# Loading one piece of a weight matrix as 120 and 8 rows, and another in one transfer, in a DMA-bound decode kernel

## The chip, the cores and the metric

The kernel runs on one core of a Trainium2 chip. The metric is the device time of one execution in microseconds (us). A profiled execution also has a span, from its first to its last instruction; the span is about 1.8 us shorter than the time.

## The reference, cut to what matters

One decode step of a gated mix: attention over a window of the cached keys and values, a small MLP, and a gate between them.

```python
# x (8, 1, 448); k_cache, v_cache (8, 8, 4096, 256); wq (448, 4096); wo (4096, 448)
q = (x @ wq)                              # 16 heads of 256
scores = q k^T / 16 over the last 1024 keys, softmax, o = p v
a = o.reshape(8, 1, 4096) @ wo            # the output projection
b = gelu(layernorm(x) @ w1 + b1) @ w2 + b2
return g * a + (1 - g) * b                # g = sigmoid(sum(x * gate_w))
```

The kernel has to read 77.7 MB of keys, values and weights from HBM, the chip's main memory. The output weights `wo` (4096 x 448 bf16, 3.67 MB) are used last.

## The kernel before

All large loads go, in a fixed order, through a ring of nine slots in SBUF, the on-chip memory; a slot is a tile of 128 partitions with 16 KB in each. One queue (SyncE) issues them. `wo` comes last, in two slots of two quarters each. A quarter has 128 rows, one per partition, of 8 columns j with 448 numbers each: 7168 B per row. `WO_PARTS` says in which pieces of j a quarter is loaded; later quarters are cut finer, so that the last matmuls wait for less.

```python
WO_PARTS = [[(0, 4), (4, 8)]] * 2 + [[(0, 4), (4, 6), (6, 8)]] * 2
...
def pump():                       # fills the ring as slots come free
    while len(slots) < min(len(plan), consumed[0] + RING):
        t = ring.tile([P, SLOT], BF16, tag="slot", name="slot")
        plan[len(slots)](t)
        slots.append(t)
...
def rows_loader(pieces):
    def load(t):
        o = 0
        for ap in pieces:
            ...                   # n = numbers per row of this piece
            dst = t[:, o : o + n]
            ...
            nc.sync.dma_start(dst, ap)
            o += n
    return load
...
wo_v = A_wo.rearrange("(q p j) n -> p q (j n)", p=P, j=NJ8)
for q in range(0, NHQ, 2):
    add(("wo", q), rows_loader(
        [wo_v[:, q + i, j0 * D : j1 * D] for i in range(2) for j0, j1 in WO_PARTS[q + i]]))
...
def project(q):                   # 24 matmuls per quarter, 3 per column j
    w = slot("wo", q - q % 2)
    for j in range(NJ8):
        o = ((q % 2) * NJ8 + j) * D
        for dst, cols in tiles(A_ps):
            nc.tensor.matmul(dst, lhsT=oP[:, j, q, :],
                             rhs=w[:, o + cols.start : o + cols.stop], ...)
```

## Time and profile before

| | before |
|---|---|
| median time, the 3 runs known at first | 190.32 us (190.27 to 190.78) |
| span of the profiled execution | 188.7 us |
| HBM read | 77.68 MB, 412 GB/s over the span |
| last landing of the output weights | 185.47 us |

The next lines are from the page of the kernel before: the span, the busy time of the compute engines (PE is TensorE's matmuls, PEld its weight loads, DVE VectorE, ACT ScalarE, POOL GpSimd), the DMA engines' busy tenths and the rate they moved in 40 equal slices, and the summary of the chain that ended last.

```profile
span 188.7 us, 2420 instructions
...
PE 134.0 (71%) x975; PEld 69.5 (37%) x975; DVE 128.0 (68%) x186; ACT 43.3 (23%) x91; POOL 5.0 (3%) x7
...
DMA  6999999999999999999999999999999999999990
GB/s 217 412 427 430 433 427 431 438 427 427 431 431 434 431 431 427 431 431 431 431 431 432 427 431 424 434 434 434 420 431 441 431 424 427 438 434 418 406 377 29
...
DMA 89%; DVE 5%; PE 4%; issue 0%; ACT 0%; SPq 0%
DMA slot<-in_A_k_cache_dram 39%; DMA slot<-in_A_wo_dram 20%; DMA slot<-in_A_v_cache_dram 20%; DMA slot<-in_B_w_dram 6%; DMA slot<-in_A_wq_dram 4%; DVE kt L358 4%; PE S L430 2%; DVE mx L442 1%; PE PO L502 1%; PE fin L532 0%; DVE ET L472 0%; DVE res L691 0%; PE mz L450 0%; DVE os__969 L517 0%; PE A_ps L673 0%
...
```

The DMA engines are busy from the second slice to the second last, at some 430 GB/s. The compute engines are not near their limit. The chain is 89% DMA.

The end of the chain in order of time (start, length, what):

```profile
...
147.47 31.34 DMA slot<-in_A_wo_dram
178.81 0.02 issue
178.83 6.65 DMA slot<-in_A_wo_dram
185.47 0.04 issue
185.52 0.33 PE A_ps L673 x5
185.84 0.03 issue
185.87 0.38 DVE res L691
```

The last landing (185.47 us) releases the last matmuls, then one VectorE instruction, then the stores. So the time is set by the slowest of the DMA engines in the last transfers. TensorE's timeline shows the same (start, length, line, shape, count, and in brackets its idle time and what ended it):

```profile
...
181.68 2.27 PE L673 MATMUL A_ps<-slot,oP 128*8 128x144 bf16 x48
184.43 0.83 PE L673 MATMUL A_ps<-slot,oP 128*8 128x160 bf16 x18 [0.48 <-DMA slot<-in_A_wo_dram]
185.52 0.30 PE L673 MATMUL A_ps<-slot,oP 128*8 128x160 bf16 x6 [0.26 <-DMA slot<-in_A_wo_dram]
```

The page gives a mean over 16 DMA engines. In the trace a transfer of 128 rows has 16 landings on its semaphore, which I take as one per engine. For the last piece of `wo` the trace has them at these times in us:

```
183.39 183.62 183.63 183.77 183.87 183.97 184.00 184.33 184.59 184.80 184.97 185.00 185.01 185.03 185.09 185.47
```

The engines finish over 2.1 us, and the last is 0.38 us behind the next. The trace's DMA packet records carry no engine number. But nearly every packet starts 3 to 4 ns before another one ends (4912 of the 4935 that start between 30 and 180 us), so they can be chained into 16 lanes, which I take for the 16 engines. Seven lanes are late (they end their data at 184.51 to 185.19 us, the others at 183.07 to 184.02 us), and they are the seven that carried one 16 KB instruction fetch each (0.88 to 0.97 us).

### The profile page before, as it was taken

What the parts mean: (1) busy time and instruction counts of PE and PEld (TensorE: products, weight loads), DVE (VectorE), ACT (ScalarE), POOL (GpSimd) and SP (SyncE); (2) the same over time, 40 slices, a digit from 0 to 9 for tenths busy, and PEclk for the clock granted to TensorE, in tenths of its full rate; (3) what the DMA queues carried; (4) which work ended last, traced back from release to release, by engine and by line L of the source; (5) the groups of instructions that cost most, each with busy time, mean ns of one, the idle gap of its engine ahead of it and who ended that gap; (6) DMA issues with size and microseconds to landing.
All of it is one profiled execution on the core that took longest, in us unless ns stands there. A gap on an engine that the chain in (4) does not pass through costs nothing.

```text
span 188.7 us, 2420 instructions
## 1 busy us (share of the span) xinstructions
PE 134.0 (71%) x975; PEld 69.5 (37%) x975; DVE 128.0 (68%) x186; ACT 43.3 (23%) x91; POOL 5.0 (3%) x7
## 2 busy tenths in 40 slices
PE   0056789795848875699758599959693999397592
PEld 0022754342414342344333153515241534144281
DVE  7841498997949492949494949585867777695210
ACT  2032400214130404022404004401240043135200
POOL 8100000000000000000000000000000000000000
PEclk9999658999996999759999657988999579999758
DMA  6999999999999999999999999999999999999990
GB/s 217 412 427 430 433 427 431 438 427 427 431 431 434 431 431 427 431 431 431 431 431 432 427 431 424 434 434 434 420 431 441 431 424 427 438 434 418 406 377 29
DMA packets 7293, 77.84 MB, mean 412 GB/s; under 512 B 993, under 2 KB 1650, under 8 KB 2546
## 3 DMA queue, kind: packets, MB, share of 16 engines
q1 hardware_dynamic: 7088, 77.67, 97.0%
q8 instruction: 7, 0.11, 0.2%
q10 hardware_dynamic: 194, 0.02, 0.1%
q14 instruction: 4, 0.03, 0.0%
HBM read 77.68 MB, written 0.01 MB: 412 GB/s over the span
## 4 chain that ended last, share of the span: by engine, by line
DMA 89%; DVE 5%; PE 4%; issue 0%; ACT 0%; SPq 0%
DMA slot<-in_A_k_cache_dram 39%; DMA slot<-in_A_wo_dram 20%; DMA slot<-in_A_v_cache_dram 20%; DMA slot<-in_B_w_dram 6%; DMA slot<-in_A_wq_dram 4%; DVE kt L358 4%; PE S L430 2%; DVE mx L442 1%; PE PO L502 1%; PE fin L532 0%; DVE ET L472 0%; DVE res L691 0%; PE mz L450 0%; DVE os__969 L517 0%; PE A_ps L673 0%
## 5 line engine op out<-in xcount | busy, mean ns | idle before, releaser
L358 DVE STREAM_TRANSPOSE kt<-slot 128x2048 int32<-128x2048 int32 x32 | 73.7, 2305 | 32.1 <-DMA slot<-in_A_k_cache_dram 32.1
L430 PE MATMUL S<-kt,qw 128*128 128x512 bf16 x256 | 70.1, 420 | 29.1 <-DVE kt L358 26.4
L430 PEld LDWEIGHTS <-qw 128*128 128x128 bf16 x256 | 26.4, 103 | 68.4 <-issue 47.1
L459 ACT ACTIVATE E<-S,nmx 128x1024 bf16<-128x1024 f32 x16 | 22.2, 1390 | 3.2 <-DVE nmx L456 3.2
L535 ACT CAST oT<-fin 128x16 bf16<-128x16 f32 x16 | 3.6, 227 | 76.3 <-PE fin L532 76.3
L502 PE MATMUL PO<-slot,ET 128*16 128x512 bf16 x256 | 19.8, 437 | 1.4 <-DMA slot<-in_A_v_cache_dram 1.4
L442 DVE TENSOR_REDUCE mx<-S 128x1 f32<-128x1024 f32 x16 | 18.9, 1184 | 0.0
L511 ACT ACTIVATE first<-PO,own 128x256 f32<-128x256 f32 x16 | 7.6, 474 | 30.1 <-PE PO L502 30.1
L424 PE MATMUL S<-place,foreign 128*128 128x512 bf16 x32 | 13.1, 410 | 0.1
L472 DVE STREAM_TRANSPOSE ET<-E 128x512 int32<-128x512 int32 x16 | 11.2, 697 | 2.2 <-ACT E L459 2.2
L450 PE MATMUL mz<-m,same 128*128 128x4 f32 x32 | 6.6, 278 | 4.1 <-ACT oT L535 4.1
L483 PEld LDWEIGHTS den<-rowsum,rowden 128*128 128x128 f32 x32 | 7.3, 232 | 3.7 <-issue 1.4
L502 PEld LDWEIGHTS <-ET 128*16 128x16 bf16 x256 | 5.5, 93 | 6.5 <-issue 3.1
L450 PEld LDWEIGHTS mz<-m,same 128*128 128x128 f32 x32 | 5.5, 211 | 6.0 <-ACT oT L535 5.3
L424 PEld LDWEIGHTS <-foreign 128*128 128x128 bf16 x32 | 3.2, 101 | 9.4 <-issue 7.6
L483 PE MATMUL den<-rowsum,rowden 128*128 128x1 f32 x32 | 5.3, 235 | 0.4 <-ACT E L459 0.4
L673 PE MATMUL A_ps<-slot,oP 128*8 128x144 bf16 (+1 forms) x96 | 4.5, 301 | 0.8 <-DMA slot<-in_A_wo_dram 0.7
L494 ACT ACTIVATE rsel<-sel,rb 128x8 f32<-128x8 f32 x16 | 4.7, 296 | 1.1 <-DVE rb L493 1.1
L415 DVE CAST qw<-qp 32x512 bf16<-32x512 f32 x4 | 2.7, 687 | 3.1 <-ACT qw L413 3.1
L293 POOL MEMSET qw<- 128x5120 bf16 x1 | 4.4, 4366 | 0.0
L391 DVE COPY qd<-qt 128x64 bf16<-128x64 bf16 x4 | 0.6, 217 | 5.1 <-PE qt L387 5.1
L444 DVE TENSOR_SCALAR m<-block,mx 128x4 f32<-128x4 f32 x16 | 3.7, 229 | 0.6
(135 smaller groups left out, 86.9 us busy)
## 6 DMA issues: line engine op xcount, KB each, us to landing
slot<-in_A_v_cache_dram SPq DMA_DIRECT2D x16, 2048.0 KB, 37.0
slot<-in_A_k_cache_dram SPq DMA_DIRECT2D x15, 2048.0 KB, 36.6
slot<-in_A_wo_dram SPq DMA_DIRECT2D x6, 448.0 KB, 31.3
slot<-in_A_wq_dram SPq DMA_DIRECT2D x1, 2048.0 KB, 7.6
slot<-in_A_k_cache_dram SPq DMA_DIRECT2D x2, 1024.0 KB
slot<-in_B_w_dram SPq DMA_DIRECT2D x1, 1568.0 KB
slot<-in_B_w_dram SPq DMA_DIRECT2D x1, 1344.0 KB, 11.8
slot<-in_A_wq_dram SPq DMA_DIRECT2D x1, 1024.0 KB
```

The source lines that it names most:

```text
L358: nc.vector.transpose(kt[:].rearrange("p c k x r -> p (c k x r)").bitcast(WORD), kn[:, hf * CH * Dh : (hf + 1) * CH * Dh].bitcast(WORD),)
L424: nc.tensor.matmul(S[u][:, cols], lhsT=foreign[:], rhs=place[:], start=True, stop=False)
L430: nc.tensor.matmul(S[u][:, cols], lhsT=qw[:, j, u, m * RQ : m * RQ + P], rhs=kt[:, :, k, :, par], start=False, stop=(k == NK - 1 and par = ...
L442: nc.vector.reduce_max(mx[:], S[u][:], axis=AXIS.X)
L450: nc.tensor.matmul(mz[:], lhsT=same[:], rhs=m4[:], start=True, stop=True)
L459: nc.scalar.activation(E[:].rearrange("p c x i -> p c i x"), S.pop(u)[:].rearrange("p (c i x) -> p c i x", i=PAIR, x=BLK), ACT.Exp, bias=n ...
L472: nc.vector.transpose(ET[:].rearrange("p c r i -> p (c r i)").bitcast(WORD), E[:].rearrange("p c x i -> p (c x i)").bitcast(WORD),)
L483: nc.tensor.matmul(den[u][:], lhsT=rowden[:], rhs=rowsum[:], start=True, stop=True)
L494: nc.scalar.activation(rsel[u][:], sel2[:], ACT.Copy, scale=rb[:])
L502: nc.tensor.matmul(PO[32 * t : 32 * t + PAIR * RQ], lhsT=ET[:, c, 0:RQ, :], rhs=vn[:, PAIR * c * Dh : PAIR * (c + 1) * Dh], start=(c < QUA ...
L511: nc.scalar.activation(first[:], PO[:, 0, :], ACT.Copy, scale=own[:, 0:1])
L673: nc.tensor.matmul(dst, lhsT=oP[:, j, q, :], rhs=w[:, o + cols.start : o + cols.stop], start=(q == 0 and j == 0), stop=(q == NHQ - 1 and j ...
```

## The change

Its intent, as I read it: the DMA engines do not finish together (2.1 us apart in the trace above). The 120-row transfer and the 8-row transfer I take to use 15 engines and 8; the cut spares the sixteenth engine its share of one piece, in the hope that this one ends last. The first quarter in one transfer keeps the number of `wo` transfers at ten.

```diff
-    WO_PARTS = [[(0, 4), (4, 8)]] * 2 + [[(0, 4), (4, 6), (6, 8)]] * 2
+    WO_PARTS = [[(0, 8)], [(0, 4), (4, 8)]] + [[(0, 4), (4, 6), (6, 8)]] * 2
...
-    def rows_loader(pieces):
+    def rows_loader(pieces, cut=None):
         def load(t):
             o = 0
-            for ap in pieces:
+            for i, ap in enumerate(pieces):
...
-                nc.sync.dma_start(dst, ap)
+                for r0, r1 in ((0, P - 8), (P - 8, P)) if i == cut else ((0, P),):
+                    nc.sync.dma_start(dst[r0:r1], ap[r0:r1])
...
-                ]
+                ],
+                cut=4 if q else None,
```

The piece that is cut is columns 4 and 5 of the last quarter (224 KB). The last piece, columns 6 and 7, stays whole.

## The prediction

> **What bounds the kernel.** DMA. The page's slice view has the 16 DMA engines at 9 tenths or more in 38 of 40 slices, mostly at 405 to 440 GB/s. The chain that ended last is 89% DMA. The output weights' landings are its last stretch, until 185.5 us; then 0.33 us of matmuls (L673), 0.38 us for the result (L691) and the stores; the span is 188.7 us.
>
> **The tail, from the packet records.** A transfer of 128 rows has 16 landings, one per DMA engine. For the last weight piece they come from 183.39 us to ... 184.97, 185.00, 185.01, 185.03, 185.09 and, alone, 185.47 us. The last matmuls need all 16: one engine is 0.38 us behind the next. I chained the packet records into 16 lanes (a packet starts 3 to 4 ns before its lane's last one ends). The seven late lanes are the seven that each carried one 16 KB instruction fetch (0.88 to 0.97 us, with slower packets around it). The latest lane also had the slowest first packet (1.69 us; most 1.0 to 1.3). Lanes never even out: the queue stays full to the end. The records do not name engines. [...]
>
> **What the change does.** [...] engine 15 is spared its 8 packets of 1792 B. Here these follow each other every 70.5 ns: with a completion record near 0.57 us. [...]
>
> First quarter in one transfer: two packets of 3584 B per row (136.5 ns each) become one of 7168 B. Estimate from 159, 309 and 611 ns for 4, 8 and 16 KB: 271 ns; with the saved completion record 0.05 us less per engine. It mainly keeps the number of weight transfers at 10. The last issue waits for an earlier completion and comes about 1 us later (near 179.9 us), with 3 us or more still queued on every engine: free. The first projection starts at 180.5 us, after its weights landed anyway. No compute instruction changes.
>
> **Worth.** All on the critical path only if engine 15 is the laggard. Then the last landing falls back to the next lane: 0.38 + 0.05 = about 0.43 us less. Otherwise: 0.05 less to 0.03 more. That the cut spares exactly engine 15, by a bit more than the lag, makes me give 70% to the first. Predicted: 190.0 us (before 190.32), 0.2% less; range 189.5 to 190.5, widened for the scatter of before (190.27 to 190.78). Chances: faster by over 2% 0.01; within 2% 0.98; slower 0.01.
>
> **What the profile would show.** Right: 15 landings for the 120-row piece and 8 for the 8-row piece; the last piece's final landing near 185.05 us and no longer alone (under 0.15 us after the next); the first projection does not wait for weights; 7168 B packets take about 271 ns. Wrong: the lone last landing stays, near 185.4 us.
>
> **What would make it wrong.** The laggard changes from run to run (slow first packets, rotating instruction fetches), so sparing one engine helps less on average; 120 rows take fewer than 15 engines; the narrower transfer slows its packets.

"Engine 15" is only my name for the engine that gets no row of the cut piece; no record carries an engine number. The sum came to 0.38 + 0.05 = 0.43 us less if that engine was the last one. Of the other case, 0.05 us less to 0.03 us more, the upper end is, less the 0.05 us, one more packet for each engine that gets one of the 8 rows besides its share of the 120, 0.076 us (an estimate from 70.5 ns to the next packet and 5.5 ns for a completion record, in the trace of before). The predicted 190.0 us, 0.32 us less, lies between the two cases.

## The result

| | before | changed |
|---|---|---|
| median of 4 runs each | 190.30 us (190.24 to 190.78) | 190.97 us (190.81 to 191.24) |
| span of the profiled execution | 188.7 us | 189.0 us |
| last landing of the output weights | 185.47 us | 185.78 us |

The ratio is 1.0031, with a 95% interval of 1.0011 to 1.0052: slower by 0.3%, clear of noise, where 0.2% less was predicted. All ratios here are the mean time of one kernel's fast runs over that of the other's of the same rounds, so not quite the ratio of the medians. (The profiled execution of before, 190.53 us, was one of its slower ones, and the changed kernel's, 190.81 us, its fastest; so the two traces differ by less than the medians.)

The same lines of the changed kernel's page:

```profile
span 189.0 us, 2420 instructions
...
PE 127.9 (68%) x975; PEld 66.4 (35%) x975; DVE 127.8 (68%) x186; ACT 43.2 (23%) x91; POOL 5.0 (3%) x7
...
DMA  6999999999999999999999999999999999999990
GB/s 223 403 427 433 428 432 440 427 420 427 444 440 413 427 440 437 413 433 433 444 433 404 433 440 440 409 433 440 437 427 416 437 440 437 406 437 426 410 353 31
...
DMA 93%; PE 4%; DVE 1%; issue 0%; ACT 0%; SPq 0%
DMA slot<-in_A_k_cache_dram 60%; DMA slot<-in_A_wo_dram 23%; DMA slot<-in_B_w_dram 6%; DMA slot<-in_A_wq_dram 4%; PE S L432 3%; DVE kt L360 1%; PE PO L504 1%; PE A_ps L675 0%; PE fin L534 0%; DVE res L693 0%; PE mz L452 0%; PE S L426 0%; ACT oT L537 0%; PE den L485 0%; SPq L119 0%
...
```

Little has moved except in the 39th slice: 353 GB/s instead of 377. The chain's end:

```profile
...
142.29 36.20 DMA slot<-in_A_wo_dram
178.49 0.02 issue
178.51 7.07 DMA slot<-in_A_wo_dram
185.58 0.04 issue
185.62 0.53 PE A_ps L675 x9
186.15 0.02 issue
186.18 0.38 DVE res L693
```

And TensorE's timeline:

```profile
...
181.56 1.98 PE L675 MATMUL A_ps<-slot,oP 128*8 128x144 bf16 x48
184.65 0.44 PE L675 MATMUL A_ps<-slot,oP 128*8 128x160 bf16 x12 [1.11 <-DMA slot<-in_A_wo_dram]
185.62 0.50 PE L675 MATMUL A_ps<-slot,oP 128*8 128x160 bf16 x12 [0.53 <-DMA slot<-in_A_wo_dram]
```

The last two waits for weights are longer (1.11 and 0.53 us instead of 0.48 and 0.26). By the landings of the trace the first of them ends with the last quarter's first piece (184.61 us) and the second with the 8 rows of the cut piece (185.58 us). The VectorE instruction after them takes 0.38 us as before. The first projection, in both kernels, did not wait for weights.

The windows of the tail show the rate. The columns are the stretch, its length, the busy time of PE, PEld, DVE, ACT and POOL with instruction counts, the granted clock, the DMA engines' busy share and, last, GB/s. Before:

```profile
...
182.00:184.00 2.00, 1.95 (x45) 1.77 (x40) 0.28 (x1) 0.00 (x0) 0.00 (x0) 0.55 0.89 346
184.00:186.00 2.00, 1.03 (x24) 0.54 (x23) 0.13 (x1) 0.00 (x0) 0.00 (x0) 1.00 0.17 66
...
```

Changed:

```profile
...
182.00:184.00 2.00, 1.54 (x42) 1.40 (x37) 0.16 (x1) 0.00 (x0) 0.00 (x0) 0.73 0.94 314
184.00:186.00 2.00, 0.82 (x24) 0.48 (x23) 0.00 (x0) 0.00 (x0) 0.00 (x0) 1.00 0.28 95
...
```

From 182 to 184 us the changed kernel moves 314 GB/s instead of 346, while its DMA engines are called busier (0.94 instead of 0.89). The packets take longer. That is directly visible in the packet records: a packet of 1792 B normally takes 74 ns, one of 3584 B 140 ns. In the changed kernel 143 of the 242 data and completion packets that start between 183 and 186 us are slow: over 80 ns with 1792 B, over 150 ns with 3584 B, or over 12 ns for a completion, which normally takes 9 ns. Most of the slow data packets take 80 to 120 ns and 175 to 250 ns. In the kernel before, none is slow in that stretch. Summed over all lanes from 181 us on, the excess of the data packets over their normal times is 5.5 us, against 0.8 us before (the latter lies next to instruction fetches). The slow packets are in all lanes that still load, also in those still at an uncut piece.

The lanes of the changed kernel also tell which one is the sixteenth engine, because only that one has no packet of the cut piece. It ended its data at 182.85 us, before every other lane; the last ended at 185.27 us. With the eight packets that it was spared (0.57 us, an estimate from 70.5 ns from one to the next) it would have ended near 183.42 us, still before all others. It carried no 16 KB instruction fetch. So the engine that was spared had nothing to be relieved of.

### The profile page after: what moved, and what is told of

The parts are those of the page before. It is cut to its first block, busy times and chain, and to the rows that moved or that the text cites. A ratio compares the mean times of both kernels' runs of the same rounds, so it can differ in the third digit from the quotient of the medians.

```text
span 189.0 us, 2420 instructions
## 1 busy us (share of the span) xinstructions
PE 127.9 (68%) x975; PEld 66.4 (35%) x975; DVE 127.8 (68%) x186; ACT 43.2 (23%) x91; POOL 5.0 (3%) x7
## 4 chain that ended last, share of the span: by engine, by line
DMA 93%; PE 4%; DVE 1%; issue 0%; ACT 0%; SPq 0%
DMA slot<-in_A_k_cache_dram 60%; DMA slot<-in_A_wo_dram 23%; DMA slot<-in_B_w_dram 6%; DMA slot<-in_A_wq_dram 4%; PE S L432 3%; DVE kt L360 1%; PE PO L504 1%; PE A_ps L675 0%; PE fin L534 0%; DVE res L693 0%; PE mz L452 0%; PE S L426 0%; ACT oT L537 0%; PE den L485 0%; SPq L119 0%
## 5 line engine op out<-in xcount | busy, mean ns | idle before, releaser
L432 PE MATMUL S<-kt,qw 128*128 128x512 bf16 x256 | 67.5, 409 | 34.7 <-DVE kt L360 31.9
L504 PE MATMUL PO<-slot,ET 128*16 128x512 bf16 x256 | 18.3, 410 | 1.5 <-DMA slot<-in_A_v_cache_dram 1.5
L485 PEld LDWEIGHTS den<-rowsum,rowden 128*128 128x128 f32 x32 | 6.5, 207 | 3.2 <-issue 1.1
L452 PEld LDWEIGHTS mz<-m,same 128*128 128x128 f32 x32 | 5.0, 195 | 5.9 <-ACT oT L537 5.3
```

The costliest lines, as they stand in the source:

```text
L432: nc.tensor.matmul(S[u][:, cols], lhsT=qw[:, j, u, m * RQ : m * RQ + P], rhs=kt[:, :, k, :, par], start=False, stop=(k == NK - 1 and par = ...
L452: nc.tensor.matmul(mz[:], lhsT=same[:], rhs=m4[:], start=True, stop=True)
L485: nc.tensor.matmul(den[u][:], lhsT=rowden[:], rhs=rowsum[:], start=True, stop=True)
L504: nc.tensor.matmul(PO[32 * t : 32 * t + PAIR * RQ], lhsT=ET[:, c, 0:RQ, :], rhs=vn[:, PAIR * c * Dh : PAIR * (c + 1) * Dh], start=(c < QUA ...
```

## The experiments

Theory A: the 120-row transfer slows the packets of all engines while it is in flight, and sparing an engine that is early gains nothing. Rivals: B, the merged first quarter and the later issues; C, chance, the laggard differing by execution; D, the 8-row transfer; later E (a cost for each odd transfer, whatever its bytes), F (a cost only in the tail) and a rival that blames the reading of the source.

In e4, theory A is taken to hold for other row counts than 128 in general. "Destination theory" stands for the supposition that the cause lies where the engines write.

### The two halves of the change, and the 8 rows

e1 has only the merged quarter:

```diff
-                cut=4 if q else None,
+                cut=None,
```

> Only the first quarter in one transfer, no cut (9 weight transfers). Theory A (the 120-row transfer is the cause: it slows the packets of every DMA engine while it is in flight): 190.2 to 190.3 us, as before or 0.05 us less; no packet of 1792 or 3584 B in the last 4 us is slower than its usual 74 or 140 ns outside lanes with an instruction fetch. Rival B (the merged transfer and the later issues are the cause): 190.9 us or more. Rival C (chance: which engine lags differs from execution to execution): 190.3 us, with another spread of the last landings than before.

e2 has only the cut:

```diff
-    WO_PARTS = [[(0, 8)], [(0, 4), (4, 8)]] + [[(0, 4), (4, 6), (6, 8)]] * 2
+    WO_PARTS = [[(0, 4), (4, 8)]] * 2 + [[(0, 4), (4, 6), (6, 8)]] * 2
```

> Only the cut into 120 and 8 rows, first quarter in two transfers as before (11 weight transfers). Theory A: 190.9 to 191.1 us, with the slow packets (about 97 ns for 1792 B, 195 ns for 3584 B) from about 183 us on in all lanes still loading, and the last landing 0.4 to 0.5 us after the last data packet. Rival B: 190.3 us, no slow packets.

e3 is the changed kernel with the piece whole and the 8-row transfer beside it:

```diff
-                for r0, r1 in ((0, P - 8), (P - 8, P)) if i == cut else ((0, P),):
-                    nc.sync.dma_start(dst[r0:r1], ap[r0:r1])
+                nc.sync.dma_start(dst, ap)
+                if i == cut:
+                    nc.sync.dma_start(t[P - 8 : P, 2 * NJ8 * D : 2 * NJ8 * D + n], ap[P - 8 : P])
```

> The changed kernel with the piece uncut (128 rows), but with the 8-row transfer kept beside it: the same 8 rows are loaded a second time, into unused columns of the same slot (result unchanged). Theory A: as e1, at most 0.1 us more for 8 packets of 1792 B, 190.2 to 190.4 us, no slow packets. Rival D (the 8-row transfer, 8 engines writing 8 neighbouring partitions, is the cause): 190.8 to 191.1 us with slow packets from the moment the 8-row packets run.

e4 cuts at 112 rows:

```diff
-                for r0, r1 in ((0, P - 8), (P - 8, P)) if i == cut else ((0, P),):
+                for r0, r1 in ((0, P - 16), (P - 16, P)) if i == cut else ((0, P),):
```

> The changed kernel with the piece cut at 112 rows: 112 and 16 rows, both over 16 engines. Theory A [...]: 190.8 to 191.1 us with slow packets, although no engine is spared. Form A2 (only the 15-engine transfer does it): 190.3 us, no slow packets.

Measured, against 11 runs of before in the same rounds (median 190.49 us):

| run | median us | ratio (95% interval) | packet excess from 181 us on, all lanes | last landing |
|---|---|---|---|---|
| e1 merge only | 190.39 | 0.9995 (0.9982 to 1.0008) | 0.6 us | 185.53 |
| e2 cut only | 191.30 | 1.0055 (1.0023 to 1.0087) | 4.3 us | 186.02 |
| e3 8 rows beside | 190.55 | 1.0002 (0.9990 to 1.0014) | 0.7 us | 185.49 |
| e4 112 and 16 | 190.77 | 1.0013 (1.0001 to 1.0025) | 2.7 us | 185.70 |

The tail windows of e2:

```profile
...
182.00:184.00 2.00, 2.00 (x57) 1.96 (x43) 0.29 (x1) 0.00 (x0) 0.00 (x0) 0.50 0.93 325
184.00:186.00 2.00, 0.77 (x20) 0.37 (x18) 0.00 (x0) 0.00 (x0) 0.00 (x0) 0.76 0.27 94
...
```

and of e3:

```profile
...
182.00:184.00 2.00, 2.00 (x51) 1.92 (x43) 0.29 (x1) 0.00 (x0) 0.00 (x0) 0.50 0.94 362
184.00:186.00 2.00, 1.52 (x26) 0.79 (x23) 0.00 (x0) 0.00 (x0) 0.00 (x0) 0.50 0.16 60
...
```

With the cut the rate from 182 to 184 us is 325 GB/s; with 8 rows beside a whole piece it is 362. The cut alone makes the loss, all of it. (One of e2's six runs took 193.30 us; without it the ratio of the means would be 1.0038. Its median is a little above the 190.9 to 191.1 us expected, e4's a little below its 190.8 to 191.1.) The merged quarter is neutral: B falls. The 8-row transfer is harmless by itself: D falls. In e4 no engine is left out (with the same row counts e8 has 16 landings for every transfer), yet packets are slow (2.7 us of excess) and the time is a little longer: so the count of 15 engines is not needed for the effect (A2 falls); a cut into 112 and 16 rows has it too. C falls as a cause, since cut and uncut kernels separate in every trace; chance in the laggard is real but small: in e1 and e3 a single lane ends its data last again, 0.40 and 0.24 us after the next, with a fetch at 102.0 and 160.2 us (in the kernel before at 72.8 us).

### The transfer by itself, sixteen times as large

To measure the disputed cost alone, e5 loads every quarter in one transfer of 128 rows, and e6, e7 and e8 cut every quarter by rows. All move the same 3.67 MB, sixteen times the cut piece.

```diff
-    WO_PARTS = [[(0, 8)], [(0, 4), (4, 8)]] + [[(0, 4), (4, 6), (6, 8)]] * 2
+    WO_PARTS = [[(0, 8)]] * 4
...
-                cut=4 if q else None,
+                cut=None,       # e5; cut=(0, 1) in e6 (120 and 8), e7 (64 and 64), e8 (112 and 16)
```

In e6 to e8 the loader's test `i == cut` also becomes `cut and i in cut`, and its row bounds are those of the run.

> Control for e6 to e8: each quarter of the output weights in one transfer of 128 rows (4 transfers of 896 KB), no cut. Slower than before only by the longer matmul tail after the last landing (24 column steps of the last quarter instead of 6 matmuls, about 1 us): 191.0 to 191.6 us. Packets of 7168 B take 272 ns as in the changed kernel, all theories alike.

> As e5, every quarter cut into 120 and 8 rows: the disputed transfer alone and 16 times as many bytes as in the change. Theory A: packets of 7168 B well above 272 ns for the whole stretch (by the 1.35 to 1.4 fold seen in the change: near 370 ns), so 2.5 to 4 us longer than e5. Rival E (the cost is at the start or end of an odd transfer, not in its bytes): about 0.6 us per cut at most and packets mostly at 272 ns, at most 1 us longer than e5.

> As e5, every quarter cut into 64 and 64 rows, all 16 engines in use. If the cause is the destination [...]: the rate falls to about half while these transfers are in flight, packets of 7168 B near 530 ns, 6 to 9 us longer than e5. If the cause is an engine count other than 16: as e5.

> As e5, every quarter cut into 112 and 16 rows, 16 engines in use in both[...]. Destination theory: slowed, less than or about as e6 (e4 showed half of the excess of the change): 1 to 3 us longer than e5. Engine-count rival: as e5.

That the rate in e7 would fall to half was supposed. The figures with it are near what half the rate would make of 272 ns a packet and of 3.67 MB at some 430 GB/s (8.5 us longer).

Measured, against 7 runs of before in the same rounds (median 190.48 us):

| run | median us | ratio to before (95% interval) | mean packet of 7168 B |
|---|---|---|---|
| e5 whole | 191.28 | 1.0038 (1.0017 to 1.0059) | 273 ns |
| e6 120 and 8 | 198.88 | 1.0441 (1.0397 to 1.0485) | 432 ns |
| e7 64 and 64 | 198.79 | 1.0434 (1.0404 to 1.0465) | 476 ns |
| e8 112 and 16 | 198.08 | 1.0402 (1.0372 to 1.0433) | 457 ns |

Windows in the middle of these transfers, first e5:

```profile
...
178.00:180.00 2.00, 0.84 (x10) 0.40 (x3) 0.48 (x1) 0.47 (x1) 0.00 (x0) 0.50 1.02 427
180.00:182.00 2.00, 2.00 (x52) 1.97 (x55) 0.00 (x0) 0.23 (x1) 0.00 (x0) 0.50 1.01 413
...
```

then e6:

```profile
...
178.00:180.00 2.00, 1.89 (x16) 0.42 (x15) 0.00 (x0) 0.00 (x1) 0.00 (x0) 0.50 0.99 251
180.00:182.00 2.00, 0.96 (x5) 0.94 (x6) 0.48 (x1) 0.47 (x1) 0.00 (x0) 0.50 0.91 240
...
```

e7:

```profile
...
180.00:182.00 2.00, 1.26 (x13) 1.23 (x16) 0.48 (x1) 0.37 (x2) 0.00 (x0) 0.50 0.99 233
...
```

and e8:

```profile
...
180.00:182.00 2.00, 0.84 (x7) 0.59 (x3) 0.48 (x1) 0.47 (x1) 0.00 (x0) 0.50 0.95 240
...
```

The rate, 413 to 427 GB/s in e5, is 233 to 251 GB/s in the others: 0.56 to 0.59 of e5's in the same window, for all three cuts alike, while their DMA engines' busy share stays at 0.91 to 0.99. e6 takes 7.6 us more than e5. That is more than twice what I had expected from the change's own packets (2.5 to 4 us); for e7 the expectation of 6 to 9 us held, though its packets are less slow than the 530 ns named; e8, expected 1 to 3 us longer than e5, takes 6.8 us more. A part of e6's loss is mere unevenness: if 120 and 8 rows use 15 and 8 engines, as the landings of the changed kernel say, eight engines get nine packets per quarter instead of eight, and four more packets at e5's 273 ns make 1.1 us (an estimate). e7 and e8 leave no engine out (16 landings for every transfer) and lose 7.5 and 6.8 us all the same. Divided by sixteen it is 0.48 us per cut piece, against 0.67 us in medians for the change. So the cost goes roughly with the bytes, and rival E (a cost per odd transfer) falls. One thing stays open: with one small piece, 112 and 16 rows (e4) lost 0.28 us in medians, well under e2's 0.81, but with sixteen times the bytes e8 loses nearly as much as e6.

### Source or destination

The row split may change two things at once: which rows an engine reads from HBM and which partitions it writes (the trace does not show which row went through which engine). e9 and e10 repeat e5 and e6 with every row read from row 0 of its quarter, so that all source addresses are alike; e11 permutes the source rows of the 120-row transfers.

```diff
-                    wo_v[:, q + i, j0 * D : j1 * D]                                   # e9, e10
+                    wo_v[0:1, q + i, j0 * D : j1 * D].to_broadcast([P, (j1 - j0) * D])
...
-                    nc.sync.dma_start(dst[r0:r1], ap[r0:r1])                          # e11
+                    src = ap[r0:r1]
+                    if r1 - r0 == P - 8:
+                        src = src.rearrange("(i j) n -> j i n", j=15)
+                    nc.sync.dma_start(dst[r0:r1], src)
```

> As e5 (whole quarters, 128 rows), but every row is read from row 0 of its quarter (wrong result on purpose): the control for e10. If reading one row from all engines is free: packets of 7168 B at 272 ns and about 191.3 us, as e5. If that alone is slow, e10 says nothing.

> As e6 (quarters cut into 120 and 8 rows), every row read from row 0 of its quarter (wrong result on purpose), so that the source addresses are the same for every engine in e9 and e10. Destination theory: still slow against e9, packets of 7168 B near 430 ns and about 7 us longer. Source rival (the 120-row order makes engines read HBM badly): as e9.

> As e6, but the 120 rows are taken from the source in another order (destination row 8i+j reads source row 15j+i and so on; wrong result on purpose)[...]. Destination theory: as e6, 198 to 200 us, packets near 430 ns. Source rival: clearly different from e6, nearer to e5's 191.3 us.

Each was run once: 191.24, 198.26 and 198.58 us; packets of 7168 B took 273, 442 and 438 ns on average. (They load wrong weights; the comparison with the reference still passed, so it is not sharp for this part.) Windows of e9, e10 and e11:

```profile
...
180.00:182.00 2.00, 2.00 (x45) 1.97 (x47) 0.00 (x0) 0.23 (x1) 0.00 (x0) 0.50 1.02 417
...
```

```profile
...
180.00:182.00 2.00, 1.28 (x13) 1.19 (x16) 0.21 (x1) 0.23 (x1) 0.00 (x0) 0.50 0.96 237
...
```

```profile
...
180.00:182.00 2.00, 0.85 (x9) 0.15 (x1) 0.48 (x1) 0.47 (x1) 0.00 (x0) 0.50 0.98 265
...
```

With one source row for all engines, 128 rows run at 417 GB/s and 120 and 8 at 237 GB/s. The source rival falls. What is left goes with the row counts, whatever rows are read; whether it lies in the engines or in the destination is not shown.

### The same cut far from the end

e12 leaves the output weights as before and cuts a piece of the same size, the second part of the first MLP weights:

```diff
-    add(("w1",), rows_loader([w1_m, w1_t]))
+    add(("w1",), rows_loader([w1_m, w1_t], cut=1))
```

> The kernel before with the same size of cut at another place: the last piece of the first MLP weights (224 KB, loaded near 14 us) as 120 and 8 rows, output weights as before. Theory A (the lost transfer time is never made up, since the queue stays full to the end): about 0.3 to 0.7 us slower than before, 190.8 to 191.2 us, although it lies 170 us before the end, with slow packets just after it and none in the last 4 us. Rival F (it hurts only in the tail, where landings are waited for one by one): 190.4 us, as before.

Measured: 191.08 us in median (190.84 to 193.52), ratio 1.0062 (1.0018 to 1.0105), against 190.37 us for before (11 runs, 190.22 to 191.70). Without the run of 193.52 us the ratio of the means would be 1.0034. The windows of before around the place:

```profile
...
18.00:22.00 4.00, 2.45 (x39) 2.25 (x37) 1.98 (x6) 1.28 (x3) 0.00 (x0) 0.74 1.02 428
22.00:26.00 4.00, 4.00 (x45) 3.86 (x44) 2.85 (x3) 1.02 (x2) 0.00 (x0) 0.50 1.01 430
...
```

and of e12:

```profile
...
18.00:22.00 4.00, 2.42 (x29) 1.99 (x27) 1.36 (x6) 1.15 (x2) 0.00 (x0) 1.00 1.04 377
22.00:26.00 4.00, 4.00 (x53) 3.98 (x52) 2.68 (x4) 1.16 (x2) 0.00 (x0) 1.00 0.99 422
...
```

The loss is at 18 to 26 us (377 instead of 428 GB/s, then 422 instead of 430), and the packet excess there is 8.9 us over all lanes, none before and almost none (0.9 us, as in the kernel before) at the end. Spread over 16 lanes, 8.9 us is 0.56 us, near the 0.7 us between the medians. So F falls: the lost time is not made up in the 160 us that follow. (I had put the load of this piece near 14 us; its packets start at 19 us.)

The experiments point to no version that beats both kernels. The merged quarter alone (e1) is the same as before within the noise.

## Why the prediction was wrong

- **What bounds the kernel: right.** DMA to the end, and 16 engines that finish 2.1 us apart.
- **How many engines the pieces use: right.** The changed kernel's trace has 15 landings for the 120 rows and 8 for the 8 rows, and one lane has no packet of the cut piece. These counts are all that this shows; by what rule they come about, and which engines they are, it does not.
- **The merged quarter: right in kind.** Packets of 7168 B take 272 ns (estimate 271). The 0.05 us expected of it cannot be told from zero in e1 (0.9995, 0.9982 to 1.0008). The last issue came at 179.6 us, and the queue was still full. The first projection did not wait.
- **"All on the critical path only if engine 15 is the laggard", given 70%: this step failed.** I inferred the laggard from the cut, not from the trace. In the changed kernel that engine ended first of all. In e10 and e11 it can be identified too: it ended the last key or value at 174.73 and 174.84 us, without a 16 KB fetch, while the lanes with such a fetch ended them at 176.2 to 177.5 us. The seven late engines of the kernel before are those with an instruction fetch (0.88 to 0.97 us, plus about 0.5 us of slower packets around it); the engine that the row counts spare had no such fetch in the changed kernel, in e10 or in e11.
- **The cost of the narrower transfer: a term that was set to zero.** It stood only among the things that could make the prediction wrong. Measured: 0.8 us between medians in e2, and 7.6 us for sixteen times the bytes. It is what turned no gain into a loss. In the profiled pair it shows as a mean end of the seven fetch lanes of 185.09 us instead of 184.74 us.
- **"The last piece's final landing no longer alone": came true for the wrong reason.** The gap shrank from 0.38 to 0.04 us, because the others became later, not because the last became earlier.

Shown: the cut alone makes the loss; it does not need 15 engines, the 8-row piece, the merge, the tail or a certain source order; in the windows shown, the rate while such transfers run is 0.56 to 0.64 of that of whole transfers (e11, with 265 GB/s, is the highest). Not shown: why. That the engines then get in each other's way where they write was only supposed. It would fit that a lane still at an uncut piece is slowed too, but the trace does not show which row went through which engine, and no run changed that with the row counts held. e7's loss (6 to 9 us expected, 7.5 measured) had been expected from the supposed half rate; it shows the size, not the cause. Also open is which engine was last in the kernel before, since its records carry no numbers.

## What to carry to other kernels

Where loads keep the DMA queue full, as here, try to keep them at 128 rows: the output weights cut into 120 and 8, 112 and 16 or 64 and 64 rows ran at 233 to 251 GB/s in the windows shown of e6 to e8, instead of 413 to 427 in e5, and in the changed kernel the slow packets of 3584 B, which belong to uncut pieces, took mostly 175 to 250 ns instead of 140. In this kernel, whose DMA queue stays full, such a loss was not made up later: the cut near 20 us cost 0.7 us between medians (e12), the one at the end 0.8 us (e2). Before relieving a resource that you believe to be last, find it in the trace, and look at GB/s and packet times rather than the busy share, which stayed at 0.91 to 0.99 in those windows.
